# Output projections put off to even out the matmul pairs of units 16 to 61, and the last product in three column parts

## Chip, cores and metric

One core of a Trainium2 chip. The metric is the device time of one execution in microseconds (us), median over the runs of one kernel. TensorE, ScalarE, VectorE, GpSimd and SyncE stand in the profile as PE (its weight loads as PEld), ACT, DVE, POOL and SP.

## The reference, cut to what matters

```python
# B=8, Sq=112, D=640, H=32, Sk=512, Dh=192, all bf16
q = (x @ wq).reshape(B, Sq, H, Dh).transpose(0, 2, 1, 3)
scores = einsum("bhqd,bhkd->bhqk", q, k_cache) * Dh ** -0.5
p = softmax(scores, axis=-1)
o = einsum("bhqk,bhkd->bhqd", p, v_cache)
return o.transpose(0, 2, 1, 3).reshape(B, Sq, H * Dh) @ wo
```

## The kernel before

The 32 heads are 8 groups of four; a group and one of 8 batches are a *unit*, so there are 64 units. In each iteration TensorE does the scores of unit i (S), the transposes of the outputs of unit i-2 (T), and the values of unit i-1 (PV). Between them it fills in pieces of the two projections: a *Q pair* (g, c) is 128 columns of a group's query projection, ten matmuls into two banks; an *O pair* (g, m) is 128 rows of a group's output projection, twelve matmuls. Each iteration has two slots for pairs, one ahead of PV and one after it. A pair can be whole in a slot, or be split into a front part and a back part in the next slot.

```python
for i in range(1, NU + 2):            # TensorE's program
    if i < NU:
        do_S(i)
    ...
    if i >= 2:
        do_T(i - 2)
    do_pair(i, 0)
    if i < NU:
        do_PV(i - 1)
    ...
    do_pair(i, 1)
```

S of a group's first unit needs that group's six Q pairs in SBUF. PV needs ScalarE's copy of the transposed outputs (`aT`), since both use bank 4. And ScalarE works in this order:

```python
def do_S(u):
    ...
    if b == 0 or u == 4:
        W(pe, aQ, q_index[g, 5, b // 4 if g == 0 else 1] + 1)   # both copies of the last Q pair
    W(pe, aEX, 4 * u)
    ...

# ScalarE
exp(i, 0); tevac(i - 2); exp(i, 1)
evac_pair(i, 0)                        # copies of a Q pair in the first slot
exp(i, 2); exp(i, 3); norm(i - 1)
evac_pair(i, 1)                        # copies of a Q pair in the second slot
```

(The last two blocks are cut; indices at the ends are left out.)

Of the kernel before, what the change touches and what calls it, by code (L numbers as in the profile page):

```python
# [666 lines left out]
def build_main(nc, x, k_cache, v_cache, wq, wo, out, flag, regs, hints):  # L667
    B, SQ, D = x.shape
    _, H, SK, DH = k_cache.shape
    assert (B, SQ, D, H, SK, DH) == (8, 112, 640, 32, 512, 192)  # L670
    NG = H // 4
    NU = NG * B
    DC = D // 128
    R = B * SQ
    MT = R // 128
    HQ = R // 2
    HO = D // 2
    HL = 384
    scale = float(DH) ** -0.5
    LO, HI = 2.0 ** -30, 2.0 ** 40  # L680
    NK, NV, NT = 3, 4, 3
# [3 lines left out]
    FULL, FRONT, BACK = range(3)  # L685
# [10 lines left out]
    o_list = [(g, m, h) for g in range(NG) for m in range(MT) for h in range(2)]  # L696
    o_index = {it: n for n, it in enumerate(o_list)}
    slot = {(i, j): None for i in range(NU + 2) for j in range(2)}

    def put(i, j, pair, part=FULL):  # L700
        assert slot[i, j] is None
        slot[i, j] = (pair, part)

    def halves(i, j, pair):
        put(i, j, pair, FRONT)
        put(i + j, 1 - j, pair, BACK)

    for g in range(NG):
        i0 = 8 * g
        if g > 0 and g < NG - 1:  # L710
            put(i0, 0, ("O", g - 1, 4))
            put(i0, 1, ("Q", g + 1, 0))
            put(i0 + 1, 0, ("O", g - 1, 5))
            halves(i0 + 1, 1, ("Q", g + 1, 1))
            put(i0 + 2, 1, ("O", g - 1, 6))
            put(i0 + 3, 0, ("Q", g + 1, 2))
            halves(i0 + 3, 1, ("Q", g + 1, 3))
            put(i0 + 4, 1, ("O", g, 0))
            put(i0 + 5, 0, ("Q", g + 1, 4))
            halves(i0 + 5, 1, ("Q", g + 1, 5))  # L720
            put(i0 + 6, 1, ("O", g, 1))
            put(i0 + 7, 0, ("O", g, 2))
            put(i0 + 7, 1, ("O", g, 3))
        elif g == 0:
            put(1, 0, ("Q", 1, 0))
            put(1, 1, ("Q", 1, 1))
            put(2, 0, ("Q", 1, 2))
            halves(2, 1, ("Q", 1, 3))
            put(3, 1, ("Q", 1, 4))
            put(4, 0, ("O", 0, 0))  # L730
            halves(4, 1, ("Q", 1, 5))
            put(5, 1, ("O", 0, 1))
            put(6, 0, ("O", 0, 2))
            put(7, 1, ("O", 0, 3))
        else:
            halves(i0, 0, ("O", g - 1, 4))
            halves(i0 + 1, 0, ("O", g - 1, 5))
            put(i0 + 2, 0, ("O", g - 1, 6), FRONT)
            put(i0 + 3, 0, ("O", g - 1, 6), BACK)
            for m in range(4):  # L740
                halves(i0 + 4 + m, 0, ("O", g, m))
            put(i0 + 8, 0, ("O", g, 4))
            put(i0 + 9, 0, ("O", g, 5))
            put(i0 + 9, 1, ("O", g, 6))
    pairs = [slot[i, j][0] for i in range(NU + 2) for j in range(2) if slot[i, j] and slot[i, j][1] != BACK]
    done_at = [slot[i, j][0] for i in range(NU + 2) for j in range(2) if slot[i, j] and slot[i, j][1] != FRONT]
    before = {p: pairs[n - 1] if n else ("Q", 0, 5) for n, p in enumerate(pairs)}
# [3 lines left out]
    assert pairs == done_at and len(pairs) == 6 * (NG - 1) + MT * NG  # L751
    assert [p for p in pairs if p[0] == "Q"] == [("Q", g, c) for g in range(1, NG) for c in range(6)]
    assert [p for p in pairs if p[0] == "O"] == [("O", g, m) for g in range(NG) for m in range(MT)]

    kt_ahead, done = [], 4
    for i in range(NU + 2):
# [4 lines left out]
    with ExitStack() as es:  # L761
# [3 lines left out]
        def sem(name):  # L765
            return es.enter_context(nc.semaphore(name))
# [46 lines left out]
        mW0 = [sem(f"mW0{j}") for j in range(DC)]  # L813
        mWQ = [sem(f"mWQ{j}") for j in range(DC)]
        mWO = [[sem(f"mWO{j}{c}") for c in range(3)] for j in range(2)]
        mOUT = [sem(f"mOUT{j}") for j in range(MT + 1)]
        XM = [(0, 2), (2, 4), (4, MT)]
        x_piece = [0, 0, 1, 1, 2, 2, 2]

        def W(eng, s, v):  # L820
            if v > 0:
                eng.wait_ge(s, v)

        def bank_of(pair, h):
            return (3, 5)[h] if pair == aside else 6 + h

        def bank_free(eng, pair, h):
            if pair == aside:
                return
            k, g, c = before[pair]  # L830
            if k == "Q":
                W(eng, aQ, q_index[g, c, h] + 1 if g else 11 + h)
            else:
                W(eng, vO, o_index[g, c, h] + 1)
# [5 lines left out]
            return -(-128 * (m + 1) // SQ) - 1  # L840

        def get_flag(eng):
            W(eng, vO, len(o_list))
            W(eng, vT, 3)
            eng.reg_load(regs[eng.engine], flag[0:1, 0:1])

        def on_tensor(pe):
# [53 lines left out]
            def do_pair(i, j):  # L901
                if slot[i, j] is None:
                    return
                (k, g, c), part = slot[i, j]
                pair = (k, g, c)
                if k == "Q":
                    if c == 0:
                        W(pe, gW, DC * g)
                    n, width, inc = DC, HQ, pQ
                else:  # L910
                    if part != BACK and 8 * g + last_unit(c) + 1 > min(i - 2 + j, NU - 2):
                        W(pe, aT, 8 * g + last_unit(c) + 1)
                    n, width, inc = 6, HO, pO
                steps = {FULL: range(n), FRONT: range(n // 2), BACK: range(n // 2, n)}[part]
                fill = FILL.get((i, j), 1)
                apart = (i, j) == (NU + 1, 1)
                for q, hs in [(q, [h]) for h in range(2) for q in steps] if apart else [(q, range(2)) for q in steps]:
                    if k == "Q":
                        w = wqs[:, g % 2, q, 128 * c:128 * (c + 1)]
                        rhs = [xT[:, q, HQ * h:HQ * (h + 1)] for h in range(2)]  # L920
                    else:
                        if c == 0 and q % 2 == 0:
                            W(pe, mWO[g % 2][q // 2], 32 * (g // 2 + 1))
                        w = oT[:, q, 128 * c:128 * (c + 1)]
                        rhs = [wos[:, g % 2, q, HL * h:HL + (D - HL) * h] if apart else wos[:, g % 2, q, HO * h:HO * (h + 1)]
                               for h in range(2)]
                    for h in hs:
                        if q == 0:
                            bank_free(pe, pair, h)
                        cuts = fill if q else 1  # L930
                        for f in range(cuts):
                            cs = slice(0, (HL, D - HL)[h]) if apart else slice(width * f // cuts, width * (f + 1) // cuts)
                            mm = (pe.matmul if h == hs[0] and f == 0 else held)(ps[:, bank_of(pair, h), cs], w, rhs[h][:, cs], q == 0,  # L933
                                                                               q == n - 1 and f == cuts - 1)
                        if q == n - 1:
                            mm.then_inc(inc, 1)
# [163 lines left out]
        def on_vector(dve):  # L1100
# [20 lines left out]
                                  rinv[:, u % 4, 0:2][:, :, None].broadcast_to([SQ, 2, DH]), op=ALU.mult).then_inc(vNM, 1)  # L1121

            def do_OE(g, m, h):
                n = o_index[g, m, h]
                W(dve, pO, n + 1)
                cs = slice(HO * h, HO * (h + 1))
                if (g, m) == (NG - 1, MT - 1):
                    cs = slice(HL * h, HL + (D - HL) * h)
                src = ps[:, bank_of(("O", g, m), h), 0:cs.stop - cs.start]
                if g == 0:  # L1130
                    ins = dve.tensor_copy(acc[:, m, cs], src)  # L1131
                else:
                    W(dve, vO, n - 2 * MT + 1)
                    ins = dve.tensor_tensor(ob[:, m, cs] if g == NG - 1 else acc[:, m, cs], src, acc[:, m, cs], op=ALU.add)  # L1134
                ins.then_inc(vO, 1)
# [12 lines left out]
            evac_x(6)  # L1148
            def do_OEs(i, j):
                if slot[i, j] and slot[i, j][0][0] == "O" and slot[i, j][1] != FRONT:  # L1150
                    for h in range(2):
                        do_OE(*slot[i, j][0][1:], h)

            for i in range(NU + 1):
# [87 lines left out]
        def on_sync(sp):  # L1242
# [53 lines left out]
            for u in range(4, NU + 1):  # L1296
                if u < NU:
                    load_k(u)
                if u - 1 >= 3:
                    load_v(u - 1)  # L1300
                for g in range(2, NG):
                    d = u - max(4, 8 * (g - 1) - 6)
                    if 0 <= d < DC:
                        load_wq(g, d)
                for g in range(1, NG):
                    d = u - (8 * g - 1)
                    if 0 <= d < 3:
                        load_wo(g, d)
            for n, (dst, src, s, count, waits) in enumerate(loads):
# [2 lines left out]
                for ws, wv in waits:  # L1312
                    W(sp, ws, wv)
                sp.dma_start(dst, src).then_inc(s, 16)  # L1314
            parts = [(m, 0, D) for m in range(MT - 1)] + [(MT - 1, 0, HL), (MT - 1, HL, D)]
            for n, (m, d0, d1) in enumerate(parts):
                W(sp, vO, 2 * (MT * (NG - 1) + m + 1) - (d1 == HL))
                sp.dma_start(out.rearrange("b s d -> (b s) d")[128 * m:128 * (m + 1), d0:d1], ob[:, m, d0:d1]).then_inc(mOUT[n], 16)
            get_flag(sp)
            for n in range(len(parts)):  # L1320
# [54 lines left out]
```

## Time and profile before

| | before |
|---|---|
| median of 3 runs | 394.29 us (393.0 to 394.81) |
| span of the profiled run | 392.2 us |
| start of S of unit 16 / 56 / 62 | 107.62 / 343.45 / 373.13 us |
| from there to the end | 19.0 us |

TensorE is the bound (busy 98% of the span, 96% of the chain that ended last), so the table gives the points in time at which it reaches a unit. The lines that carry this are in the prediction.

### The profile page before, as it was taken

The page shows a single profiled execution, that of the slowest core. Times are in us where ns is not written, and L with a number is a line of the kernel's source. Part 1 is how long each engine was busy: PE and PEld are TensorE (multiplying, and loading weights), DVE is VectorE, ACT ScalarE, POOL GpSimd, SP SyncE. Part 2 cuts the span into 40 slices and gives each one's busy share as a digit, 9 for nine tenths or more (in the row PEclk, how much of TensorE's full clock was granted, in tenths as well). Part 3 has the DMA queues.
Part 4 walks back from the last instruction along what each step waited for, and adds up shares of the span by engine and source line. Part 5 has one row for each costly group of instructions (what it writes and reads, how often), then busy time and mean ns, then how long its engine had stood idle before and what let it go on. Part 6 is the DMA issues. An engine that isn't in the chain of part 4 may idle for free.

```text
span 392.2 us, 19832 instructions
## 1 busy us (share of the span) xinstructions
PE 385.1 (98%) x8833; PEld 242.8 (62%) x8286; DVE 283.2 (72%) x506; ACT 250.4 (64%) x550; POOL 152.8 (39%) x352
## 2 busy tenths in 40 slices
PE   8999989999999999999999999999999999998997
PEld 3556665665666666566566566666566666666664
DVE  1665687677777788786687676876678677789735
ACT  3767765776665774666755766566765766667562
POOL 5542553335433445135443255333354233234331
PEclk9999999999999999999999999999999999999999
DMA  8999999999999999899999899989999789989712
GB/s 264 376 371 368 342 325 337 355 349 344 337 317 330 356 336 330 290 301 345 325 329 297 268 321 360 326 277 315 286 344 296 222 299 300 352 278 313 251 39 70
DMA packets 88584, 120.00 MB, mean 306 GB/s; under 512 B 9776, under 2 KB 88496, under 8 KB 88496
## 3 DMA queue, kind: packets, MB, share of 16 engines
q1 hardware_dynamic: 88496, 118.72, 90.9%
q8 instruction: 68, 1.11, 1.2%
q14 instruction: 20, 0.16, 0.1%
HBM read 117.54 MB, written 1.15 MB: 303 GB/s over the span
## 4 chain that ended last, share of the span: by engine, by line
PE 96%; DMA 1%; issue 1%; DVE 0%; SPq 0%; ACT 0%
PE ps L933 22%; PE ps L972 22%; PE ps L858 22%; PE ps L954 21%; PE ps L983 6%; PE ps L892 2%; DMA wqs<-in_wq_dram 1%; PE ps L877 1%; SPq L1314 0%; PE ps L897 0%; PE ps L854 0%; DVE kt L1111 0%; DVE acc L1131 0%; ACT oT L1069 0%; ACT pT L1052 0%
## 5 line engine op out<-in xcount | busy, mean ns | idle before, releaser
L1111 DVE STREAM_TRANSPOSE kt<-kr 128x384 int32<-128x384 int32 x256 | 195.2, 871 | 12.0 <-DMA kr<-in_k_cache_dram 12.0
L1052 ACT ACTIVATE pT<-ps 128x448 bf16<-128x448 f32 x256 | 130.8, 561 | 84.6 <-PE ps L954 84.3
L954 PEld LDWEIGHTS ps<-qT,kt 32*128 32x128 bf16 x6144 | 77.1, 93 | 31.3 <-issue 23.7
L933 PE MATMUL ps<-wos,oT 128*128 128x320 bf16 (+2 forms) x342 | 93.2, 299 | 0.0
L972 PE MATMUL ps<-vm,pT 128*128 128x193 bf16 x768 | 91.5, 247 | 1.0 <-ACT oT L1069 0.8
L858 PE MATMUL ps<-wos,oT 128*128 128x320 bf16 x330 | 91.2, 299 | 0.0
L954 PE MATMUL ps<-qT,kt 32*128 32x112 bf16 x6144 | 87.5, 208 | 1.9 <-issue 1.7
L1231 POOL TENSOR_SCALAR bad<-rinv 112x4 f32<-112x4 f32 x64 | 14.6, 228 | 188.9 <-DVE rinv L1117 188.8
L1214 POOL COPY vm<-vs 128x1152 int32<-128x1152 int32 x64 | 73.5, 1148 | 25.4 <-issue 17.7
L972 PEld LDWEIGHTS ps<-vm,pT 128*128 128x128 bf16 x768 | 67.9, 97 | 22.1 <-ACT oT L1069 11.6
L933 PE MATMUL ps<-xT,wqs 128*128 128x448 bf16 x210 | 74.0, 352 | 0.0
L858 PE MATMUL ps<-xT,wqs 128*128 128x448 bf16 x210 | 73.9, 352 | 0.0
L1059 ACT ACTIVATE os<-ps,rinv 112x192 bf16<-112x192 f32 x128 | 47.8, 435 | 28.1 <-DVE rinv L1117 28.1
L972 PE MATMUL ps<-vs,pT 128*128 128x193 bf16 x256 | 62.6, 245 | 0.0
L933 PEld LDWEIGHTS ps<-wos,oT 128*128 128x128 bf16 x342 | 33.2, 97 | 43.1 <-issue 35.8
L1036 ACT ACTIVATE qT<-ps 128x448 bf16<-128x448 f32 x96 | 47.8, 554 | 18.8 <-PE ps L933 13.3
L1134 DVE TENSOR_TENSOR acc<-ps,acc 128x320 f32<-128x320 f32 x84 | 37.3, 486 | 27.1 <-PE ps L933 27.1
L1069 ACT ACTIVATE oT<-ps 128x672 bf16<-128x672 bf16 x64 | 46.4, 725 | 2.1 <-PE ps L983 2.1
L1117 DVE RECIPROCAL rinv<-ps 112x4 f32<-112x4 f32 x64 | 11.1, 174 | 48.7 <-PE ps L972 48.7
L933 PEld LDWEIGHTS ps<-xT,wqs 128*128 128x128 bf16 x210 | 20.4, 97 | 34.0 <-issue 28.9
L1120 DVE TENSOR_TENSOR os<-ps,rinv 112x384 bf16<-112x384 f32 x64 | 35.7, 558 | 7.4 <-DVE rinv L1117 0.5
L1207 POOL COPY wqs<-wqr 128x384 bf16<-128x384 bf16 x70 | 33.2, 507 | 4.8 <-DMA wqr<-in_wq_dram 4.8
(44 smaller groups left out, 154.6 us busy)
## 6 DMA issues: line engine op xcount, KB each, us to landing
kr<-in_k_cache_dram SPq DMA_DIRECT2D x256, 192.0 KB, 4.1
vs<-in_v_cache_dram SPq DMA_DIRECT2D x256, 192.0 KB, 4.0
wos<-in_wo_dram SPq DMA_DIRECT2D x48, 160.0 KB, 4.4
wqr<-in_wq_dram SPq DMA_DIRECT2D x35, 192.0 KB, 5.5
wqs<-in_wq_dram SPq DMA_DIRECT2D x5, 192.0 KB, 4.6
out_dram<-xs SPq DMA_DIRECT2D x6, 160.0 KB, 1.8
xs<-in_x_dram SPq DMA_DIRECT2D x2, 320.0 KB, 3.3
xs<-in_x_dram SPq DMA_DIRECT2D x1, 480.0 KB, 6.0
```

The source lines that it names most:

```text
L858: return pe.add_instruction(mybir.InstMatmult(name=nc.get_next_instruction_name(), engine=mybir.EngineType.PE, ins=[pe.lower_ap_or_imm(rhs ...
L933: mm = (pe.matmul if h == hs[0] and f == 0 else held)(ps[:, bank_of(pair, h), cs], w, rhs[h][:, cs], q == 0, q == n - 1 and f == cuts - 1)
L954: mm = pe.matmul(ps[:, a, SQ * t:SQ * (t + 1)], kt[u % NT][p, t, c // 2, :, c % 2], qT[g % 2][p, c, SQ * b:SQ * (b + 1)], start=(c == 0), ...
L972: mm = pe.matmul(pv[:, k, e, 0:DH + 1], pT[u % 2][:, a, t, :], src[:, a, v0:v0 + DH + 1], start=(t == 0), stop=(t == 3), skip_group_check= ...
L1036: act.activation(qT[g % 2][:, c, HQ * h:HQ * (h + 1)], ps[:, bank_of_Q0(n) if g == 0 else 6 + h, 0:HQ], ACTF.Copy).then_inc(aQ, 1)
L1052: act.activation(pT[u % 2][:, a, :, 0:SQ], ps[:, a, 0:4 * SQ].rearrange("p (t q) -> p t q", t=4), ACTF.Exp, scale=scale).then_inc(aEX, 1)
L1059: ins = act.activation(os_[u % 2][:, DH * (2 + e):DH * (3 + e)], pv_of(u)[0:SQ, 1, e, 0:DH], ACTF.Copy, scale=rinv[:, u % 4, 2 + e:3 + e])
L1069: act.activation(oT[:, :, SQ * b:SQ * (b + 1)].rearrange("p (k c) q -> p k c q", k=2), src.rearrange("p k (c q) -> p k c q", c=3), ACTF.Co ...
L1111: dve.transpose(dst, src).then_inc(vKT, 1)
L1120: dve.tensor_tensor(os_[u % 2][:, 0:2 * DH].rearrange("p (e d) -> p e d", e=2), pv[0:SQ, 0, :, 0:DH], rinv[:, u % 4, 0:2][:, :, None].broa ...
L1134: ins = dve.tensor_tensor(ob[:, m, cs] if g == NG - 1 else acc[:, m, cs], src, acc[:, m, cs], op=ALU.add)
L1214: gp.tensor_copy(vm[u % NM][:].rearrange("p a (t w) -> p a t w", w=RW)[:, :, :, 0:DH].bitcast(I32), vs[u % NV][:, :, 32:32 + 3 * DH].rearr ...
```

## The change

The intent: units 56 to 63 hold half a pair or one pair each, while those ahead hold one and a half or two; the change puts O pairs off so that units 16 to 61 have one and a half each (two in units 48 and 55). The last product, 640 columns wide, goes from 384 + 256 columns and two stores to 320 + 192 + 128 and three.

```diff
-        if g > 0 and g < NG - 1:
+        if g == 1:
             (the places of group 1, unchanged)
-        else:
-            halves(i0, 0, ("O", g - 1, 4))
-            halves(i0 + 1, 0, ("O", g - 1, 5))
-            ... (the places of the last group)
+    late = [("O", g, m) for g in range(1, NG) for m in range(MT)][4:]
+    stream = []
+    for g in range(2, NG - 1):
+        qs = [("Q", g + 1, c) for c in range(6)]
+        for n in range(7 if g == NG - 2 else 6):
+            stream += [late.pop(0)] + qs[n:n + 1]
+    stream += late[:-3]
+    counts = [3] * (NU - 16)                      # half pairs in each unit
+    for i in (NU - 16, NU - 9):
+        counts[i - 16] += 1
+    for i in (NU - 2, NU - 1):
+        counts[i - 16] -= 1
+    ... (fills the slots from the stream, splitting a pair where a unit's count asks for it)
+    wo_round = [0] + [8 * g - 1 for g in range(1, NG)]   # output weights are loaded later to match
+    ...
-    HL = 384
+    EDGE = (0, 320, 512, D)
-                for q, hs in [(q, [h]) for h in range(2) for q in steps] if apart else ...
+                for q, hs in [(q, [h]) for h in range(3) for q in steps] if apart else ...
     (likewise the banks, evacuations, stores and counts of the last product)
```

What it does to five units, with f and b for a front and a back part, first slot | second slot:

| unit | before | changed |
|---|---|---|
| 20 | Q3.3b \| O2.0 | O2.0 \| Q3.3f |
| 21 | Q3.4 \| Q3.5f | Q3.3b \| O2.1 |
| 22 | Q3.5b \| O2.1 | Q3.4 \| O2.2f |
| 23 | O2.2 \| O2.3 | O2.2b \| Q3.5 |
| 24 | O2.4 \| Q4.0 | O2.3 \| Q4.0f |

More of the change, by code (lines that the diff above doesn't have):

```diff
@@ L734, in build_main @@
             put(7, 1, ("O", 0, 3))
-        else:
-            halves(i0, 0, ("O", g - 1, 4))
-            halves(i0 + 1, 0, ("O", g - 1, 5))
-            put(i0 + 2, 0, ("O", g - 1, 6), FRONT)
-            put(i0 + 3, 0, ("O", g - 1, 6), BACK)
-            for m in range(4):
-                halves(i0 + 4 + m, 0, ("O", g, m))
-            put(i0 + 8, 0, ("O", g, 4))
-            put(i0 + 9, 0, ("O", g, 5))
-            put(i0 + 9, 1, ("O", g, 6))
+    late = [("O", g, m) for g in range(1, NG) for m in range(MT)][4:]
[10 more added lines that the diff above has]
+        counts[i - 16] -= 1
+    assert sum(counts) == 2 * len(stream)
+    back = None
+    for i, count in enumerate(counts, 16):
+        for j in range(2):
+            if back:
+                put(i, j, back, BACK)
+                back, count = None, count - 1
+            elif count >= 2 and not (j == 0 and count == 2):
+                put(i, j, stream.pop(0))
+                count -= 2
+            elif count:
+                back = stream.pop(0)
+                put(i, j, back, FRONT)
+                count -= 1
+        assert count == 0
+    assert not stream and back is None
+    put(NU, 0, late[-3])
+    put(NU + 1, 0, late[-2])
+    put(NU + 1, 1, late[-1])
     pairs = [slot[i, j][0] for i in range(NU + 2) for j in range(2) if slot[i, j] and slot[i, j][1] != BACK]
@@ L753, in build_main @@
     assert [p for p in pairs if p[0] == "O"] == [("O", g, m) for g in range(NG) for m in range(MT)]
+    wo_round = [0] + [8 * g - 1 for g in range(1, NG)]
+    for g in range(2, NG):
+        wo_round[g] = max(wo_round[g], 5 + max(i for (i, j), it in slot.items() if it and it[0] == ("O", g - 2, MT - 1)))
     kt_ahead, done = [], 4
@@ L815, in build_main @@
         mWO = [[sem(f"mWO{j}{c}") for c in range(3)] for j in range(2)]
-        mOUT = [sem(f"mOUT{j}") for j in range(MT + 1)]
+        mOUT = [sem(f"mOUT{j}") for j in range(MT + 2)]
         XM = [(0, 2), (2, 4), (4, MT)]
@@ L824, in bank_of @@
         def bank_of(pair, h):
-            return (3, 5)[h] if pair == aside else 6 + h
+            return (3, 5)[h] if pair == aside else (6, 7, 4)[h]
         def bank_free(eng, pair, h):
-            if pair == aside:
+            if pair == aside or h == 2:
                 return
@@ L842, in get_flag @@
         def get_flag(eng):
-            W(eng, vO, len(o_list))
+            W(eng, vO, len(o_list) + 1)
             W(eng, vT, 3)
@@ L916, in do_pair @@
                 apart = (i, j) == (NU + 1, 1)
-                for q, hs in [(q, [h]) for h in range(2) for q in steps] if apart else [(q, range(2)) for q in steps]:
+                for q, hs in [(q, [h]) for h in range(3) for q in steps] if apart else [(q, range(2)) for q in steps]:
                     if k == "Q":
@@ L924, in do_pair @@
                         w = oT[:, q, 128 * c:128 * (c + 1)]
-                        rhs = [wos[:, g % 2, q, HL * h:HL + (D - HL) * h] if apart else wos[:, g % 2, q, HO * h:HO * (h + 1)]
-                               for h in range(2)]
+                        rhs = [wos[:, g % 2, q, e0:e1] for e0, e1 in zip(*((EDGE, EDGE[1:]) if apart else ((0, HO), (HO, D))))]
                     for h in hs:
@@ L931, in do_pair @@
                         for f in range(cuts):
-                            cs = slice(0, (HL, D - HL)[h]) if apart else slice(width * f // cuts, width * (f + 1) // cuts)
+                            cs = slice(0, EDGE[h + 1] - EDGE[h]) if apart else slice(width * f // cuts, width * (f + 1) // cuts)
                             mm = (pe.matmul if h == hs[0] and f == 0 else held)(ps[:, bank_of(pair, h), cs], w, rhs[h][:, cs], q == 0,
@@ L1123, in do_OE @@
             def do_OE(g, m, h):
-                n = o_index[g, m, h]
+                n = o_index[g, m, 0] + h
                 W(dve, pO, n + 1)
@@ L1127, in do_OE @@
                 if (g, m) == (NG - 1, MT - 1):
-                    cs = slice(HL * h, HL + (D - HL) * h)
+                    cs = slice(EDGE[h], EDGE[h + 1])
                 src = ps[:, bank_of(("O", g, m), h), 0:cs.stop - cs.start]
@@ L1150, in do_OEs @@
                 if slot[i, j] and slot[i, j][0][0] == "O" and slot[i, j][1] != FRONT:
-                    for h in range(2):
+                    for h in range(3 if (i, j) == (NU + 1, 1) else 2):
                         do_OE(*slot[i, j][0][1:], h)
@@ L1305, in on_sync @@
                 for g in range(1, NG):
-                    d = u - (8 * g - 1)
+                    d = u - wo_round[g]
                     if 0 <= d < 3:
@@ L1314, in on_sync @@
                 sp.dma_start(dst, src).then_inc(s, 16)
-            parts = [(m, 0, D) for m in range(MT - 1)] + [(MT - 1, 0, HL), (MT - 1, HL, D)]
+            parts = [(m, 0, D) for m in range(MT - 1)] + [(MT - 1, e0, e1) for e0, e1 in zip(EDGE, EDGE[1:])]
             for n, (m, d0, d1) in enumerate(parts):
-                W(sp, vO, 2 * (MT * (NG - 1) + m + 1) - (d1 == HL))
+                W(sp, vO, 2 * MT * (NG - 1) + (2 * (n + 1) if n < MT - 1 else n + MT))
                 sp.dma_start(out.rearrange("b s d -> (b s) d")[128 * m:128 * (m + 1), d0:d1], ob[:, m, d0:d1]).then_inc(mOUT[n], 16)
```

## The prediction

> **What bounds the kernel now.** I read the busy table, then the chain that ended last, then the same four stretches as windows, then TensorE's instructions in order of time. In the page's first and fourth parts the reader is to see that TensorE is busy nearly all the time and is nearly the whole chain:
>
> ```profile
> PE 385.1 (98%) x8833; PEld 242.8 (62%) x8286; DVE 283.2 (72%) x506; ACT 250.4 (64%) x550; POOL 152.8 (39%) x352
> ...
> PE 96%; DMA 1%; issue 1%; DVE 0%; SPq 0%; ACT 0%
> ```
>
> The windows are units 16 to 55, units 56 to 61, units 62 and 63, and the tail. Columns: stretch, its length, then busy time of PE, PEld, DVE, ACT, POOL, clock, DMA share, GB/s. In the first there is no idle TensorE left (235.78 of 235.83 us); in the second it is idle 1.8 us; the clock is full throughout.
>
> ```profile
> 107.62:343.45 235.83, 235.78 (x5442) 148.17 (x5083) 178.57 (x315) 153.15 (x340) 90.80 (x203) 1.00 0.95 313
> 343.45:373.13 29.68, 27.89 (x769) 19.53 (x738) 25.58 (x46) 19.00 (x42) 10.15 (x23) 1.00 0.87 275
> ```
>
> From the starts of the matmuls in the timeline I take the cost of each piece: scores of one unit (S) 1.29 us, transposes of the outputs (T) 0.31, values (PV) 1.35, an O pair 1.63, a Q pair 1.89, and 0.10 more where TensorE goes from the unit's second slot to the next S. A half pair costs half (O 0.82), so splitting is free. In units 16 to 55 every unit adds up to these within 0.06, but for unit 23 (0.2 over): moving pairs about inside this stretch can't gain. All removable loss lies after it, of two kinds, seen in the chain in order of time (start, length, what; units 59 to 61):
>
> ```profile
> 359.70 0.14 PE ps L858
> 359.84 0.03 issue
> 359.87 1.52 PE ps L972 x16
> 361.39 0.30 PE ps L954 x13
> 361.69 1.18 issue
> 362.88 1.21 PE ps L954 x82
> ...
> 367.64 0.30 PE ps L954 x14
> 367.95 0.49 issue
> 368.44 0.57 PE ps L954 x30
> ```
>
> First, PV appears as 1.52 instead of 1.35 after a half pair: it starts 0.18 to 0.19 us late. Second, S stops twice after 13 or 14 of 96 matmuls, where the program waits for nothing: S takes 2.69 and 1.99 instead of 1.29 us, a loss of 1.40 + 0.70 = 2.1 us.
>
> The first is a wait for ScalarE. PV needs the copy of the transposed outputs, which ScalarE does after the first exponential of the unit:
>
> ```profile
> 344.83 0.54 ACT L1052 ACTIVATE pT<-ps 128x448 bf16<-128x448 f32 x1 [1.94 <-PE ps L954]
> 345.27 0.72 ACT L1069 ACTIVATE oT<-ps 128x672 bf16<-128x672 bf16 x1
> 345.88 0.55 ACT L1052 ACTIVATE pT<-ps 128x448 bf16<-128x448 f32 x1
> ```
>
> S ended at 344.74, the copy at 345.99, PV began at 346.05: never under 1.32 us from the end of S. T and half an O pair fill 0.31 + 0.82 = 1.13 of that, so 0.19 is lost. A back part of a Q pair (three of five steps, 1.14) or a full pair hides it. Units 56 to 63 all have half an O pair there: 8 x 0.19 = 1.5 us.
>
> The second is the fetch of instructions. Counting TensorE's records, the two stops are at records 16065 and 16321, exactly 256 apart, and both have the remainder 193 by 256; so has unit 23's loss. The queue that fetches them:
>
> ```profile
> q8 instruction: 68, 1.11, 1.2%
> ```
>
> That is 16 KB a packet, about 256 instructions of TensorE. Against the boundaries, a packet starts 0.1 to 3.8 us after the boundary before and takes about 1.0; the stops ended 1.3 and 1.5 us after a landing. So a block needs up to 3.1 + 1.0 + 1.4 = 5.5 us (an estimate from these), and TensorE went through the blocks before in 4.1 to 4.9 us. In units 16 to 55 it takes 5.4 to 6.5.
>
> [...] the 1.52 of PV counts as busy and holds a wait; so I used start-to-start times. [...] Pairs here share banks 6 and 7, with S, T or PV between; the trace shows 0.3 us of such waits in all.
>
> **The change part by part.** The work is the same: 42 Q and 56 O pairs, and as many S, T and PV. Only places move, so I wrote out both tables of slots from the two programs.
>
> 1. Units 56 to 61 go from 1 or 0.5 pairs to 1.5. The price is paid back one for one in units 16 to 55, where TensorE is saturated. Gain from the move itself: 0.
> 2. Fetch stops. Units of 1.5 pairs have some 262 TensorE instructions in 5.7 us, so a block lasts about 5.5, just what a late packet needs. The 2.1 us should mostly go; I leave 0.3 for short stops. With unit 23's 0.2: gain 2.0.
> 3. The wait for ScalarE's copy. In the new table a half O pair stands before PV in units 19, 23, 27, 31, 35, 39, 43, 47, 52, 57, 59, 61, 62, 63: 14 instead of 8 times. 6 x 0.19 = 1.1 us lost.
> 4. A new wait, the largest term. In the old table the last Q pair of a group is finished in the first slot of the unit two before its first use (units 22, 30, 38, 46, 54). In the new one Q pairs 3.5, 4.5, 5.5, 6.5 stand in the second slot of units 23, 31, 39, 47, and S of units 24, 32, 40, 48 is TensorE's very next work. It waits until ScalarE has copied both halves of that pair. What this costs is seen after the Q pair of unit 19, which ended at 128.92:
>
> ```profile
> 128.73 0.35 PE L858 MATMUL ps<-xT,wqs 128*128 128x448 bf16 x1
> 128.92 0.42 PE L972 MATMUL ps<-vm,pT 128*128 128x193 bf16 x3
> ...
> 128.93 0.98 ACT L1036 ACTIVATE qT<-ps 128x448 bf16<-128x448 f32 x2 [0.51 <-PE ps L933]
> ```
>
> ScalarE starts 0.01 after the slot's end, both copies take 0.98, and 0.06 to 0.07 pass from a copy's end to the matmul that waited (345.99 to 346.05). So S starts 1.06 after the pair, not 0.10: 0.96 each, 4 x 0.96 = 3.8 us lost. Nothing on TensorE's program stands between to fill it. Group 7's last Q pair is in unit 55's first slot, with PV and an O pair (3.0 us) behind it, so it costs nothing.
> 5. VectorE. In units 56 to 61 it has four transposes of 0.87, 0.17 + 0.56 for the norm and three evacuations of 0.49 for each 1.5 pairs: 3.48 + 0.73 + 1.47 = 5.7 us against 5.5 to 5.7 of TensorE. Followed by hand the evacuations come just in time; I add 0.1.
> 6. The tail. The last 256 columns become 192 and 128. VectorE's last evacuation shrinks from 0.43 to about 0.30 (it did 320, 384 and 256 columns in 0.49, 0.56 and 0.43), and six extra weight loads add a few hundredths on TensorE. But SyncE issues one store after another, 0.4 to 0.5 us apart; the third store then issues at about the time at which the second did. Sum 0, within 0.15.
> 7. Weight loads of the output matrix go later by up to 5 rounds; each still lands two units ahead. 0.
>
> Sum: -2.0 + 1.1 + 3.8 + 0.1 = +3.0 us. 394.3 + 3.0 = 397.3.
>
> **The rivals.** (a) The intended gain: all late loss vanishes and nothing new appears. It is the 2.1 + 1.5 us of above at most, so 390.7; against it stands the dependence of S on the Q pair right ahead of it. (b) The wait for Q is partly covered, because ScalarE takes up the first half early: the two copies then still end one copy (0.5 us) after the last matmul; at least 0.45 each remains, and the time would be 395.3. Against it: unit 19's copies began at the slot's end, though the first half had been ready a little before. (c) Transfers or VectorE become the bound: units 16 to 61 run at 5.7 us instead of 5.9, so DMA must deliver 14.55 MB in 8 units, 320 GB/s instead of 308. The first fifth of the trace shows 340 to 376 GB/s with the same loads, and no wait for keys after the start; I don't expect it. If it came, 399 to 401. (d) Fetch stops stay or come up elsewhere, because the blocks' time is at their limit: up to 2 us more, 399.
>
> **Range and chances.** Between (b) with no stops and (d): 394.3 to 399.3. Faster by 2% would need 7.9 us, more than twice all the removable loss; slower by 2% would need terms 3 and 4 plus another 5 us.
>
> **What would show it right or wrong.** In the changed profile: units 24, 32, 40 and 48 begin S about 1.06 us after the end of the Q pair (0.10 before), with ScalarE's copy of qT as the releaser (a new row of some 4 us over four times); PV starts late by 0.19 in 14 units; no stop of over 0.5 us inside S at 256-record boundaries after unit 56; the tail from the last PV to the end is 9.4 us as before. I am wrong if S starts at once after Q pairs, or if units 16 to 55 take more than 5.69 us on average plus these waits.

The "such waits" are waits for a bank: once, a pair's weight load behind VectorE's evacuation, 0.3 us. For the packets of queue 8: 68 of 16 KB against 8833 + 8286 = 17119 matmuls and weight loads is 252 for each, near the 256 between two stops. That TensorE stops for these packets is an inference here; experiments 6 and 7 test it. The few hundredths for weight loads in step 6 are an estimate; the measured difference, 0.02 us, stands with steps 5 to 7 below.

## The result, and the profile after

The changed kernel takes 399.17 us, median of 6 runs (398.08 to 400.02), against 394.31 us of the kernel before in the same rounds. The ratio is 1.0122 with a 95% interval of 1.0097 to 1.0148. (A ratio is the mean time of one kernel's fast runs over that of the other's of the same rounds, so not quite the ratio of the medians.) It is clearly a loss, of some 4.8 us, where +3.0 was forecast.

The page of the changed kernel, its first and fourth parts. TensorE has hardly more work, but ScalarE has come into the chain:

```profile
PE 387.4 (98%) x8839; PEld 243.6 (61%) x8292; DVE 285.4 (72%) x507; ACT 251.5 (63%) x550; POOL 152.7 (38%) x352
...
PE 96%; ACT 1%; DMA 1%; issue 1%; DVE 0%
```

The windows of units 16 to 55 and 56 to 61, columns as in the prediction. The idle time has changed sides: before, 0.05 and 1.8 us; now 4.6 us in the first and 0.1 in the second:

```profile
108.20:344.36 236.16, 231.55 (x5393) 145.32 (x5058) 176.33 (x307) 154.42 (x340) 90.87 (x203) 1.00 0.94 307
344.36:377.90 33.54, 33.45 (x817) 21.98 (x764) 29.84 (x55) 19.24 (x42) 10.78 (x25) 1.00 0.83 270
```

The row of the waits view that is new (who waited <- for whom: us in total, times, longest), and the chain in order of time (start, length, what) at the change from unit 31 to 32. In this kernel L978 is S, L996 PV, L957 and L883 are the pairs, and L1060 is ScalarE's copy of a Q pair; "issue" is time without a wait that the profile shows:

```profile
PE ps L978 <- ACT qT L1060: 3.6, 4, 0.9
```

```profile
201.18 0.19 PE ps L883
201.37 0.20 PE ps L957
201.57 0.02 issue
201.59 0.21 ACT qT L1060
201.80 0.23 issue
202.03 0.55 ACT qT L1060
202.58 0.05 issue
202.62 1.36 PE ps L978 x96
```

The last matmul of Q pair 4.5 starts at 201.37; S of unit 32 starts at 202.62, after both of ScalarE's copies. The start of each S and Q in the timeline puts the loss at 1.00 us in unit 23 and 0.95 in 31, 39 and 47. PV is late (it waits for `aT`) by 0.17 to 0.20 us in exactly the 14 units named in the prediction.

The stops that the change was to be rid of are gone from units 60 and 61, but others have come, two of them here (unit 24, ahead of a Q pair; unit 52, inside S):

```profile
158.51 1.35 PE ps L996 x16
159.86 0.49 issue
160.35 0.36 PE ps L957
```

```profile
320.19 0.75 PE ps L978 x51
320.94 0.27 issue
321.21 0.74 PE ps L978 x45
```

All four are at a TensorE record with remainder 193 by 256, as the stops before were; I call them *fetch stops* (step 2 of the prediction). From the starts of the matmuls these two cost 0.66 and 0.48 us, with 0.27 in unit 37 and 0.22 in unit 7: 1.6 us, where before had 2.3.

The difference of the spans of the two profiled runs, 397.03 - 392.17 = 4.86 us, is made up as follows, from start-to-start times: four waits for Q +3.85; six more late PVs +1.12; fetch stops -0.7; first S later +0.37; from S of unit 62 to the end 19.13 against 19.04, +0.09. That makes 4.73.

### The profile page after: what moved, and what is told of

It is laid out like the page before. It is cut to its first block, busy times and chain, and to the rows that moved or that the text cites. A ratio compares the mean times of both kernels' runs of the same rounds, so it can differ in the third digit from the quotient of the medians.

```text
span 397.0 us, 19847 instructions
## 1 busy us (share of the span) xinstructions
PE 387.4 (98%) x8839; PEld 243.6 (61%) x8292; DVE 285.4 (72%) x507; ACT 251.5 (63%) x550; POOL 152.7 (38%) x352
## 4 chain that ended last, share of the span: by engine, by line
PE 96%; ACT 1%; DMA 1%; issue 1%; DVE 0%
PE ps L996 22%; PE ps L957 22%; PE ps L883 21%; PE ps L978 21%; PE ps L1007 6%; PE ps L917 2%; DMA xs<-in_x_dram 1%; PE ps L879 1%; ACT qT L1060 1%; PE ps L902 1%; PE ps L922 0%; DVE kt L1135 0%; DVE acc L1155 0%; ACT oT L1093 0%; ACT pT L1076 0%
## 5 line engine op out<-in xcount | busy, mean ns | idle before, releaser
L1135 DVE STREAM_TRANSPOSE kt<-kr 128x384 int32<-128x384 int32 x256 | 197.2, 873 | 8.1 <-DMA kr<-in_k_cache_dram 8.1
L978 PEld LDWEIGHTS ps<-qT,kt 32*128 32x128 bf16 x6144 | 77.2, 93 | 34.5 <-issue 20.6
L957 PE MATMUL ps<-wos,oT 128*128 128x320 bf16 (+2 forms) x348 | 93.4, 297 | 0.0
L996 PE MATMUL ps<-vm,pT 128*128 128x193 bf16 x768 | 91.5, 247 | 1.2 <-ACT oT L1093 0.8
L978 PE MATMUL ps<-qT,kt 32*128 32x112 bf16 x6144 | 87.7, 208 | 4.2 <-ACT qT L1060 3.6
L883 PE MATMUL ps<-wos,oT 128*128 128x320 bf16 x330 | 91.4, 299 | 0.0
L996 PEld LDWEIGHTS ps<-vm,pT 128*128 128x128 bf16 x768 | 67.4, 97 | 23.0 <-ACT oT L1093 12.9
L957 PE MATMUL ps<-xT,wqs 128*128 128x448 bf16 x210 | 74.0, 352 | 0.5 <-issue 0.5
L883 PE MATMUL ps<-xT,wqs 128*128 128x448 bf16 x210 | 73.9, 352 | 0.0
L996 PE MATMUL ps<-vs,pT 128*128 128x193 bf16 x256 | 62.6, 245 | 0.0
L1060 ACT ACTIVATE qT<-ps 128x448 bf16<-128x448 f32 x96 | 47.6, 550 | 21.8 <-PE ps L957 17.0
L957 PEld LDWEIGHTS ps<-wos,oT 128*128 128x128 bf16 x348 | 33.5, 97 | 41.0 <-issue 33.4
L957 PEld LDWEIGHTS ps<-xT,wqs 128*128 128x128 bf16 x210 | 20.4, 97 | 36.8 <-issue 32.4
```

What stands on the lines that cost most here:

```text
L883: return pe.add_instruction(mybir.InstMatmult(name=nc.get_next_instruction_name(), engine=mybir.EngineType.PE, ins=[pe.lower_ap_or_imm(rhs ...
L957: mm = (pe.matmul if h == hs[0] and f == 0 else held)(ps[:, bank_of(pair, h), cs], w, rhs[h][:, cs], q == 0, q == n - 1 and f == cuts - 1)
L978: mm = pe.matmul(ps[:, a, SQ * t:SQ * (t + 1)], kt[u % NT][p, t, c // 2, :, c % 2], qT[g % 2][p, c, SQ * b:SQ * (b + 1)], start=(c == 0), ...
L996: mm = pe.matmul(pv[:, k, e, 0:DH + 1], pT[u % 2][:, a, t, :], src[:, a, v0:v0 + DH + 1], start=(t == 0), stop=(t == 3), skip_group_check= ...
L1060: act.activation(qT[g % 2][:, c, HQ * h:HQ * (h + 1)], ps[:, bank_of_Q0(n) if g == 0 else 6 + h, 0:HQ], ACTF.Copy).then_inc(aQ, 1)
L1135: dve.transpose(dst, src).then_inc(vKT, 1)
```

## The experiments

Ten runs, all correct. The line numbers shift a little with each edit: pairs stand at L934, L957 or L959, S at L955, L978 or L980. Each job has its own runs of the kernel before on its chip, so I compare within a job, and ratios across jobs. Of the four kernels of the first job, the one with the old tail proved equal to the changed kernel and stands for it there.

**1. S waits for one copy only.** S of a group's first four batches reads only the first half of the columns:

```diff
-                if b == 0 or u == 4:
-                    W(pe, aQ, q_index[g, 5, b // 4 if g == 0 else 1] + 1)
+                if b % 4 == 0:
+                    W(pe, aQ, q_index[g, 5, b // 4] + 1)
```

> The changed kernel, but S of a group's first unit waits only for the half of the last Q pair that it reads (columns 0 to 447), and the fifth unit for the other half. Theory (S behind the Q pair waits for both of ScalarE's copies, 0.96 us four times): one copy fewer to wait for, 0.96 becomes about 0.47 in units 24, 32, 40, 48, the time 1.9 us under the changed kernel (about 397.3). Rival (the wait is one for the pair's end or for a bank, not for the second copy): stays at 0.95, time unchanged at 399.2.

396.84 us, ratio to before 1.0082 (1.0055 to 1.0109); with the old tail in the same job 1.0130. The difference is 1.9 us by the ratios (2.2 by the medians), as expected, though each ratio has an interval of some 1.1 us either way; the chain says it more sharply. The same place in the chain as above has one copy now, and the next S starts 0.05 us after it:

```profile
203.69 0.20 PE ps L957
203.89 0.02 issue
203.91 0.55 ACT qT L1060
204.46 0.05 issue
204.51 1.36 PE ps L978 x96
```

The loss is 0.51 to 0.56 us in each of the four units, where it was 0.95 to 1.00. So the wait is for ScalarE's copies, one by one.

**2. Last two pairs of a group exchanged.**

```diff
             stream += [late.pop(0)] + qs[n:n + 1]
+        if g < NG - 2:
+            stream[-2:] = stream[:-3:-1]
```

> The changed kernel, with the last two pairs of groups 2 to 5 in exchanged order (Q 3.5 before O 2.2 and so on): the last Q pair is split over units 22 and 23 and an O pair stands between it and S of unit 24. Theory: the four waits of 0.96 us go (3.8 us), and in units 23, 31, 39, 47 a back part of a Q pair instead of an O pair stands before PV, so four waits of 0.19 go too (0.8 us): 4.6 us under the changed kernel, about 394.6. Rival (the time was lost by the even pace, to fetch stops, transfers or VectorE, and the waits of S only hide it): the waits go, others come up, time within 2 us of 399.2.

393.94 us, ratio 1.0008 (0.9980 to 1.0036): 4.8 us under the old-tail kernel of the same job (1.0130) by the ratios, where 4.6 was expected. With O 2.2 between Q 3.5 and S of unit 24, S follows at once:

```profile
153.53 0.14 PE ps L959
153.67 0.14 PE ps L885
153.81 1.29 PE ps L980 x96
```

The rival, that the pace itself was lossy and the wait only hid it, falls: nothing of the size came up elsewhere (the stops of this profile sum to 0.3 us).

**3. The old tail on the changed kernel.**

```diff
-    EDGE = (0, 320, 512, D)
+    EDGE = (0, 384, D)
     (and the counts of banks, semaphores and evacuations that go with two parts)
```

> The changed kernel with the old tail: last product in two parts of 384 and 256 columns, two stores. Theory: the tail is neutral, within 0.2 us of 399.2, and from the end of the last PV to the end of the kernel 9.3 to 9.5 us either way. Rival: the third store and the six added weight loads cost; then this is 0.3 to 0.5 us faster than the changed kernel.

399.04 us, ratio 1.0130 (1.0105 to 1.0155), against 1.0122 of the changed kernel. These intervals are too wide for a rival of 0.3 to 0.5 us; the profiles decide it: from S of unit 62 to the end 19.02 us here and 19.13 in the changed kernel's, so the tail is neutral within 0.1 us.

**4. Only Q pairs split.** Same count of pairs in each unit, another order:

```diff
-    for g in range(2, NG - 1):
+    for g in range(2, NG - 2):
         qs = [("Q", g + 1, c) for c in range(6)]
-        for n in range(7 if g == NG - 2 else 6):
-            stream += [late.pop(0)] + qs[n:n + 1]
+        for n in (0, 3):
+            os = [late.pop(0) for _ in range(3)]
+            stream += [os[0], qs[n], os[1], qs[n + 1], qs[n + 2], os[2]]
+    (units 48 to 55 in like manner, seven O pairs)
```

Units 20 to 23 are then O2.0 | Q3.3f, Q3.3b | O2.1, Q3.4 | Q3.5f, Q3.5b | O2.2.

> The changed kernel with another order of the pairs in units 16 to 55 (O Q O, then Q Q O, repeated), still one and a half pairs a unit, so that only Q pairs are split and the last Q pair of a group is done before PV of the unit ahead of its first use. Theory: no wait of S for Q (3.8 us) and no late PV in nine units (1.7 us); left are 5 late PVs and the fetch stops: 5.5 us under the changed kernel, 393.2 to 394, thus level with the kernel before or a little faster. Rival (the even pace itself is what costs): no better than the exchanged order, 394.6 or more, with more fetch stops at 256-record boundaries.

393.05 us, ratio 0.9977 (0.9950 to 1.0003): 6.0 us under the old-tail kernel by the ratios, 5.5 expected. In the profile the late PVs are down to units 57, 59, 61, 62 and 63, and no S waits for Q. Run again in a third job it had 0.9965 (below).

**5. Whole O pairs from unit 56 on,** on top of that (the cut leaves out that the counts now end at unit 55):

```diff
+    tail, stream = stream[-11:], stream[:-11]
+    for i in range(NU - 8, NU):
+        put(i, 0, tail.pop(0))
+        if i in (NU - 8, NU - 6, NU - 4):
+            put(i, 1, tail.pop(0))
```

> The order that splits only Q pairs in units 16 to 55, and from unit 56 on whole O pairs only: two in units 56, 58, 60, one in the first slot of the other five. Theory: the five late PVs that are left (0.19 each) go, 0.95 us under the run that splits only Q pairs, about 392.1 and 1.3 us under the kernel before, unless the fetch stops come back in the units of one pair (4.7 us each, a block of 256 records in about 4.9): the next packet then has to come early, as there is less time; up to 1 us back. Rival (late PV costs nothing, it is made up by the next wait): no gain over the run that splits only Q pairs.

390.73 us against 394.43, ratio 0.9913 (0.9884 to 0.9943): better than the 392.1 expected, by more than late PVs can explain; the repeat below makes the excess smaller.

**6. and 7. The blocks of instructions shifted.** Both kernels, before and changed, got 64 matmuls of one column (`SHIFT` is 64) between the warm-up matmuls and TensorE's next wait, ahead of all the work:

```diff
+            for j in range(SHIFT):
+                held(ps[:, 7, 0:1], wt[:], wt[:, 0:1], True, True)
             W(pe, gI, 1)
             W(pe, vI, 1)
```

> The kernel before with 64 matmuls of one column put in at the start, where TensorE waits for its first transfer. Theory (the stops are the fetch of the next 256 instructions): any stop is again at a record with remainder 193 by 256, which is now work of 64 records earlier in the program, so not 13 or 14 matmuls into S of units 60 and 61 but at PV of the unit before or near it, or not at all when the packets come in time. Rival (something in S itself, keys or a bank): the stops stay inside S of units 60 and 61, at remainder 1. Time as before, plus up to 1 us at the start.

One run, 394.29 us, at the full clock, its state unknown. TensorE's two stops in units 59 and 60 are again at records 16065 and 16321, now inside an O pair and two matmuls into PV, not in S:

```profile
360.71 0.14 PE ps L859
360.85 0.30 issue
361.15 0.30 PE ps L934
...
365.74 0.34 PE ps L973 x2
366.08 0.46 issue
366.55 0.49 PE ps L973 x4
```

> The changed kernel with the same 64 matmuls put in at the start. Theory: the four waits of S in units 24, 32, 40, 48 stay at 0.95 us and the 14 late PVs at 0.19; stops of other sizes are at remainder 193 by 256, at other work than in the changed kernel's own profile (not at the Q pair of unit 24's second slot). Rival: unit 24's stop of 0.66 us ahead of that Q pair stays where it is, as a wait for a bank or for the weights of Q would.

One run, 402.61 us, state unknown, so the time is not compared. The stop of unit 24 is gone; stops came inside PV of units 17 and 19 (0.95 and 1.91 us) and S of units 27 and 44 (0.44 and 0.26), and the gaps are at records 5057, 5569, 7617 and 11969, all with remainder 193 by 256. The four waits for Q stay at 0.95 to 0.99 us and the late PVs at 0.18 to 0.20. In both kernels the stops move with the count of instructions and not with the work. With one packet of queue 8 (kind "instruction" in the page) for each 256 records, I take them for the fetch of the next block. Their sum in this one execution is 3.7 us with the 0.12 in unit 7. Only the profile of experiment 1 has as much, 3.75 us (1.06, 0.16, 0.41, 1.21 and 0.91 in units 7, 10, 11, 24 and 28, all with remainder 193); it was the slowest of that kernel's six runs, 399.66 against a median of 396.84.

**8. to 10. The even pace on trial.** The kernel before with whole O pairs in units 56, 57 and 60 to 63 and nothing else changed, beside the kernels of 4 and 5 again, on one chip:

```diff
-            halves(i0, 0, ("O", g - 1, 4))
-            halves(i0 + 1, 0, ("O", g - 1, 5))
+            put(i0, 0, ("O", g - 1, 4))
+            put(i0 + 1, 0, ("O", g - 1, 5))
...
-                halves(i0 + 4 + m, 0, ("O", g, m))
+                put(i0 + 4 + m, 0, ("O", g, m))
```

> The kernel before, units 16 to 55 untouched, with the O pairs of units 56, 57 and 60 to 63 whole in the first slot instead of half and half. Theory: six late PVs of 0.19 us go, 1.1 us faster than before (about 393.2); units 58 and 59 keep theirs, and the fetch stops stay about 2 us, as those units are as short as before. Rival (the gain of the run with whole late pairs needs the even pace): no change, or slower through longer stops.

392.19 us against 394.26, ratio 0.9962 (0.9918 to 1.0006; one of the six runs took 396.38). The gain is 1.5 us by the ratio and 2.1 by the medians, where 1.1 was expected; the interval does not exclude zero. In its profile PV is late in units 58 and 59 alone. The profiled run had a stop of only 0.25 us in unit 60 and none in 61, at the same short units as before.

> The order that splits only Q pairs, again, to stand beside the run with whole late pairs on one chip. Theory: 0.3 to 1.0 us under the kernel before (three late PVs fewer, 0.57 us, and about as many fetch stops).

392.73 us, ratio 0.9965 (0.9932 to 0.9997).

> The order with whole late pairs, again. Theory: five late PVs of 0.19 us fewer than the run that splits only Q pairs, so 0.95 us under it; a gap of over 1.5 us between the two, as the two separate jobs gave, would mean that fetch stops differ as well. Rival: the gap was one of chips and shrinks to the 0.95 or less.

391.63 us, ratio 0.9924 (0.9893 to 0.9954): 1.1 us under its neighbour by the medians, 1.6 by the ratios, where the separate jobs gave 2.3 and 2.5. So a good part of that gap lay in the job, the chip or the runs (not told apart); what is left fits 0.95. The rival in experiment 8, that this gain needs the even pace, is not settled: this kernel is 1.5 us under that of 8 by the ratios, of which two late PVs explain 0.4, with intervals wider than the rest. In its profile TensorE is not idle for a moment from S of unit 56 to S of unit 62, and no PV is late:

```profile
338.80:371.74 32.94, 32.94 (x819) 22.27 (x765) 29.33 (x54) 18.50 (x40) 9.77 (x21) 1.00 0.86 274
```

This version beats both kernels: 0.8 to 0.9% under the kernel before, and some 2% under the changed one by the quotient of ratios of two jobs (0.9924 / 1.0122 = 0.980; the two were not run side by side).

## Why the prediction was right or wrong

*TensorE is the bound and moving pairs gains nothing by itself* (step 1): right. In every profile the pieces S, T, PV, O and Q cost the same (from start to start in both kernels, where nothing is waited for, 1.29, 0.31, 1.35, 1.63 and 1.89 us).

*Fetch stops: gain 2.0* (step 2): this is the step that was mis-sized. The profiled runs had 2.3 us of them before and 1.6 after, a gain of 0.7. The stops did leave units 60 and 61, and came up in units 7, 24, 37 and 52, as rival (d) said they could. Blocks that last 5.3 to 5.8 us without their stop had late packets too: in units 24, 37 and 52 the packet started (times of queue 8's packets in the packed trace) 4.06, 3.21 and 3.91 us after the boundary, had landed 0.99 to 1.10 us later, and 1.29 to 1.33 us after that TensorE went on. With stops of 0.66, 0.27 and 0.48 us these blocks lasted 6.49, 5.53 and 6.22. The estimate of 5.5 us for a block took 3.1 us for the start of the packet; with the latest start that the prediction itself lists, 3.8, it is 6.2, more than a block of 1.5 pairs lasts. And I took the stops of one profile as a fixed cost of short units. They vary from run to run: in the profiles of the two kernels and of their shifted versions they sum to 2.3, 1.6, 0.9 and 3.7 us, and one kernel (experiments 5 and 10) had 0.5 in one profile and 1.9 in the other.

The kernel with even pace and no waits for Q (experiments 4 and 9) is 0.9 and 1.4 us under before (0.9977, 0.9965); three late PVs fewer explain 0.57 of it, so the even pace itself is worth about 0.3 to 0.8 us, with intervals of 1.0 and 1.3 us either way: not clear of zero.

*Late PV, 6 x 0.19* (step 3): right to the unit; 1.12 measured; experiment 4 removed nine of them, and in its profile none of the nine is late.

*S waits for the last Q pair, 4 x 0.96* (step 4): right; 3.85 measured, shown by halving it (1) and by removing it (2). Rival (b), that half is covered, was wrong for the change, and is just what experiment 1 made of it.

*VectorE 0.1, tail 0, weight loads 0* (steps 5 to 7): the tail is right (3). In the chain the last product takes 1.77 us with 18 matmuls against 1.75 with 12, VectorE's last evacuation 0.29 against 0.43, and the last three stores are issued 0.37 and 0.48 us apart, where the old kernel's last two were 0.52 apart. In units 56 to 61 the start-to-start times show no loss but the three late PVs, so VectorE cost nothing there, and no wait of TensorE for output weights appears in the profile. Nor did rival (c) come: in units 16 to 61 the changed profile shows no wait of TensorE for a transfer.

The rest of the excess, 0.37 us, is a later start of the first S. It lies ahead of anything that the change touches, and between the unshifted profiles that start moves from 12.7 to 14.7 us. So +3.0 became +4.8: 1.3 us by the fetch term, 0.4 by the start. The range held, at its upper edge: the fetch term missed in the direction of rival (d), and the later start was luck, bad here, that no step had foreseen.

One sign of being wrong that the prediction named did come: units 16 to 55 took more than 5.69 us on average plus the waits. They took 236.16 us, less 3.85 and 9 late PVs of 0.19 that is 5.76 for each. Of the 3 us in all, 1.4 are fetch stops; the rest is a slip, as 5.69 leaves out the two half pairs more in units 48 and 55 (some 1.7 us). Other slips, without weight for the sum: (b) with no stops gives some 395, not the 394.3 of the range; being slower by 2% needs the whole sum of +3.0 plus another 5 us, while terms 3 and 4 alone need 3; blocks in units 16 to 55 last 5.0 to 6.5 us, not 5.4 to 6.5; and 340 to 376 GB/s holds only for part of the first fifth, where two slices show 325 and 337 and the first 264.

Open: why a packet sometimes starts up to 4.5 us (experiment 1) after its block was begun. The loads that keep the DMA engines at a share of 0.94 in units 16 to 55 (changed kernel) are a guess; no run here varied them. Nor is it shown why the boundary at record 6849, in unit 24, stopped for 0.4 to 1.2 us in eight of the ten unshifted profiles. Five of the experiments' profiles (1, 4, 5, 8 and 9) also have a wait of 0.2 to 1.2 us in unit 8, where Q 2.0 waits for GpSimd's reordered weights; it lies in a part that no edit touches, and I have not followed it up. In experiment 1's profile, unit 43 also lost 0.57 us to VectorE, behind keys that landed late.

## What to carry to other kernels

On TensorE, busy 98% of the span here, moving pairs did not change the sum of the work: an O pair cost 1.63 us and a Q pair 1.89 wherever they stood. Look instead at what each moved piece now stands *directly ahead of*. The result of a Q pair, which ScalarE must copy before S reads it, needed other work in between: S began 1.05 to 1.11 us after the end of the pair, and an O pair (1.63 us, experiment 2) or PV with an O pair (3.0 us) hid it. Before a stop that no semaphore explains is booked as a gain, compare several profiles, and see whether its place counts in instructions or in work.

Figures beside that:

- In the kernel before, from unit 8 on, a block of 256 TensorE records lasts 4.1 to 6.5 us. Stops of 0.1 to 1.9 us at the boundaries sum to between 0.9 and 3.7 us in the two kernels and their shifted versions, under 1% of the time.
- Queue 8 has one packet for each 256 records, nearly all landing within the block before. In the kernel before a packet takes mostly about 1.0 us (0.88 to 1.95), and at the stops of the two kernels TensorE goes on 1.3 to 1.6 us after it landed.
- Two banks sufficed for the pairs: no wait of TensorE's matmuls for a bank in units 16 to 61 of the changed profile. What cost 0.95 to 1.00 us in units 23, 31, 39 and 47 was an evacuation whose reader came next in program order. From the end of a ScalarE copy to the start of the matmul that waited it is 0.05 to 0.09 us.
